# One change to a fused attention and two-MLP kernel: the weights' sign bit, the opening's dates, and one block's transposes

## The chip, the cores and the metric

One Trainium2 chip, one core. The time is the device time of one execution in microseconds (us); the kernel before takes 892.35 us, the median of three runs (892.18 to 892.69).

## What is computed

Sliding-window attention over q, k, v of shape 4 x 8 x 576 x 64 in float32, then two MLPs on the 2304 x 512 result. The weights arrive as float64 and all arithmetic is float32.

```python
# attention: window 64, causal
scores = q @ k.T / 8; scores outside 0 <= i - j < 64 are -1e9
x = softmax(scores) @ v                       # to 2304 x 512
g = max(x @ w_in, 0) + log1p(exp(-abs(x @ w_in)))     # softplus, d_ff 2048
x = g @ w_out
y = (sigmoid(x @ w_gate) * (x @ w_val)) @ w_out2      # d_ff 1536
```

## The kernel before, in words

**Tiling.** The tokens of the first MLP come in five blocks of 512, 384, 384, 512 and 512 (`BLOCKS1`, L21). Attention is done in groups of 64 queries with their 128 keys, all 8 heads at once; block 0 has eight groups, block 1 six. While the first MLP works on block b, the attention of block b + 1 is done between its matmuls. The second MLP runs afterwards over two halves of 768 + 768 tokens with a seven-product (Strassen-like) scheme (L512, L541).

**Precision.** A float32 operand is split into a high part (a rounded fp32r copy) and a low part (the difference), and each product is three matmuls (`mm3`, L405 to L408).

**Weights.** A float64 weight arrives as two 32-bit words. `w_scale` (L160) reads the high word as a float32 and multiplies it by 2^-112 on ScalarE, which moves the exponent into range; `w_shift` (L163) shifts left by 3 on VectorE, which loses the sign; `w_sign` (L167) ors the sign bit of the high word back in on VectorE; `w_low` (L172) ors in the top 3 bits of the low word. `w_hi` (L177, ScalarE) and `w_lo` (L184, VectorE or GpSimd) make the split. The first two weights are converted singly (128x512), later ones in pairs (128x1024).

**Attention.** `att_scores` (L282, TensorE), `att_max` (L294, VectorE), `att_exp` (L310, ScalarE), `att_sum` (L320, VectorE), `att_norm` (L328, GpSimd). Then the probabilities have to be turned so that keys lie on partitions. Near groups (`att_transpose` L334, `att_copy` L364) do it with four TensorE transposes into PSUM and a copy by ScalarE or VectorE. Far groups (`att_blocks` L344, `att_send` L351, `att_fetch` L356) do it with VectorE's transposes of 32x32 blocks, one DMA of 256 KB to DRAM and four DMAs of 64 KB back, all on SyncE's queue. `FAR = 2` (L26) says that blocks 2, 3 and 4 are far; blocks 0 and 1 are near. `att_values` (L381), `att_hi` and `att_lo` (L393, L399) end a group; from block 1 on two groups share one of these.

**Order.** TensorE's order is a list of slots (L601 to L626): projection and output products in turn. Everything else is an event with a slot and a rank (`at`, L631). From the start up to the second MLP a planner (`lead_in`, L957) puts all events in order: it gives each a due time, worked back from what needs it (L971 to L983), then at each step takes, among the events that could start within a window of the soonest one, the one with the earliest due time (L1009). The window is `NEAR` before `OPEN` (34 us, the planned start of the first projection) and `SLACK` after. The eight groups of block 0 are due 2.9 us apart, ending at `OPEN` (L979). The order is fixed when the kernel is built: each engine takes its instructions in that order and waits for semaphores. `warm` (L412) are idle bf16 matmuls that are placed while TensorE waits in the opening; the first projection comes behind all of them (L909).

Of the kernel before, what the change touches and what calls it, by code (L numbers as in the profile page):

```python
# [9 lines left out]
F32 = mybir.dt.float32  # L10
# [3 lines left out]
AF = mybir.ActivationFunctionType  # L14
ALU = mybir.AluOpType
# [7 lines left out]
LAG = 2  # L23
LEAD = 7
COMBO0, COMBO = 36, 9.8
FAR = 2  # L26
TWO = 1
RG = 1.1
HURRY = 1.0
SLACK, NEAR = 0.15, .3  # L30
OPEN = 34.0
FLYING, SWITCH, MARGIN, FLIP, LATE = 10, 1.3, 1.5, 6.0, 2.0
EITHER, HALVES = (("pool", 1.29), ("dve lock", 0.69)), (("pool", 0.75), ("dve lock", 0.42))
# [9 lines left out]
def tile_kernel(ctx: ExitStack, tc: tile.TileContext, qk, vt, w1, w2, wg, wv, wo, out):  # L43
# [20 lines left out]
    nc = tc.nc  # L64
# [50 lines left out]
    pair_t, raw_t, bits_t, w_t = {}, {}, {}, {}  # L115

    def pair(slot, turn, dtype, *shape):
        key = slot // 2, turn
        if key not in pair_t:
            pair_t[key] = wpool.tile([P, 2, *shape], dtype, tag=f"w{slot // 2}", name=f"w{slot // 2}", bufs=1)  # L120
        return pair_t[key]

    def size(i):
        return 2 if 1 < i < WO_AT else 1
# [13 lines left out]
    def raw(i, k):  # L138
        r = raw_t[i - i % 2].rearrange("p c (n two) -> p c n two", two=2)
        return r[:, i % 2:i % 2 + size(i), :, k]  # L140

    def bits(i):
        if i == 1:
            bits_t[i] = bits_t["first"][:, 1:]
        if i not in bits_t:
            u, n = i // 2, size(i)
            if u < 3:
                t = main.tile([P, 2, DM], U32, tag="g", name="bits", bufs=GB)
                bits_t.setdefault("first", t)
            elif 4 <= u < 14:  # L150
                slot = 14 + u % 4 // 2 if u < 12 else 15
                t = pair(2 * slot, -20 - u // 2, U32, 2 * DM)[:, u % 2].rearrange("p (c n) -> p c n", c=2)
            else:
                t = main.tile([P, 2, DM], U32, tag="bits", name="bits", bufs=1)
            bits_t[i] = t[:, :n]
        return bits_t[i]
# [1 line left out]


    def w_scale(i):  # L160
        nc.scalar.activation(out=bits(i).bitcast(F32), in_=raw(i, 1).bitcast(F32), func=AF.Copy, scale=2.0 ** -112)

    def w_shift(i):  # L163
        t = bits_t[i]
        nc.vector.tensor_scalar(out=t, in0=t, scalar1=3, scalar2=None, op0=ALU.logical_shift_left)

    def w_sign(i):  # L167
        t = bits_t[i]
        nc.vector.scalar_tensor_tensor(out=t, in0=raw(i, 1), scalar=0x80000000, in1=t, op0=ALU.bitwise_and,
                                       op1=ALU.bitwise_or)  # L170

    def w_low(i):  # L172
        t = bits_t[i]
# [71 lines left out]
    NG0 = BLOCKS1[0] // Q  # L245
# [128 lines left out]
    def both(g):  # L374
        return (g - 1, g) if grp_block[g][0] >= TWO else (g,)
# [255 lines left out]
    def at(slot, order, fn, *args):  # L631
        events[slot].append((order, len(events[slot]), fn, args))
# [28 lines left out]
    def attention(g, t, far):  # L661
        at(t, 20, att_scores, g)
        at(t + 1, -30, att_max, g)
        at(t + 2, -30, att_exp, g)
        near, odd = g < NG0, g % 2
        at(t + 4 - near, -33, att_sum, g)
        at(t + 4 - near, -32, att_norm, g)
        if far:
            at(t + 5 + 2 * odd, -31, att_blocks, g)
            at(t + 6 + 2 * odd, -61, att_send, g)  # L670
            at(t + 9 + 2 * odd, -61, att_fetch, g)
            e = t + 13
        else:
            e = t + 6 if near else t + 8
            at(e - 2, 21, att_transpose, g)
            at(e - 1, -31, att_copy, g)
        at(e - 4, -59, v_load, g)
        if ends(g) == g:
            at(e, 22, att_values, g)
            at(e + 1, -29, att_hi, g)  # L680
            at(e + 1, -28, att_lo, g)

    for b in range(1, NB1):
        s0, s1 = pos[m1_proj, b - 1, 0], pos[m1_proj, b, 0]
        ng, g0 = BLOCKS1[b] // Q, starts1[b] // Q
        for j in range(ng):
            far = b >= FAR
            first = -3 if far else 9
            t = s0 + first + (s1 - s0 - (14 if far else 15 + first)) * (j // 2) // max(ng // 2 - 1, 1)
            attention(g0 + j, t, far)  # L690
            at(t - 4, -60, qk_load, g0 + j)


    def weight(i, t):
        for k in range(size(i)):
            at(t - 2, 50, w_load, i + k)
        at(t, -20, w_scale, i)
        at(t + 1, -20, w_shift, i)
        at(t + 1, -19, w_sign, i)
        at(t + 1, -18, w_low, i)  # L700
        at(t + 2, -20, w_hi, i)
        for k in range(size(i)):
            at(t + 2, -19, w_lo, i + k)

    for i in (0, 1, *range(2, len(seq1), 2)):
        weight(i, i + LAG - (i < 3) * (3 - i) - LEAD)
# [3 lines left out]
    def used_last(slot):  # L710
        return max(pos[m1_proj if kind == "w1" else m1_out, NB1 - 1, f]
                   for (kind, f), _ in seq1[slot - slot % 2:slot - slot % 2 + 2])

    for f in range(NF2):
        t, i = COMBO0 + int(COMBO * f), len(seq1) + 2 * f
        at(t - 2, -60, w_load, i)
        at(t - 1, -60, w_load, i + 1)
        at(t, -20, w_scale, i)
        at(t + 1, -20, w_shift, i)
        at(t + 1, -19, w_sign, i)  # L720
        at(t + 1, -18, w_low, i)
        at(t + 3, -15, c_sums, f)
        at(t + 4, -15, c_sum4, f)
        for k, part in enumerate(("a", "v", "x", "s4")):
            at(t + 2 + k, -14, c_hi, f, part)
            at(t + 2 + k, -13, c_lo, f, part)
            at(t + 6 + k, -61, c_send, f, part)
    for f in range(NF2):
        i = WO_AT + f
        t = end + (-7, -1)[f] if f < 2 else pos[m2_out, 0, f - 2, 0] - 1  # L730
        t0 = t - 8
        assert used_last(place[i]) < t < pos[m2_out, 0, f, 0] - 4, (f, used_last(place[i]), t, pos[m2_out, 0, f, 0])
        at(t0, -60, w_load, i)
        at(t, -20, w_scale, i)
        at(t + 1, -20, w_shift, i)
        at(t + 2, -20, w_sign, i)
        at(t + 3, -20, w_low, i)
        at(t + 4, -20, w_hi, i)
        at(t + 4, -19, w_lo, i)
    at(last + 4, -62, wc_load, 0, 0)  # L740
    at(end, -62, wc_load, 0, 1)
    for s in range(NS2):
        t = last + 2 if s == 0 else pos[m2_prod, s - 1, 3, 0]
# [5 lines left out]
    for k in range(7):  # L749
        for kc in range(2):  # L750
            t = max(used_last(2 * k + kc) + 1, last + 18 + k)
# [26 lines left out]
    first = -int(RG * NG0) - 6  # L778
    for g in range(NG0):
        t = int(first + RG * g)  # L780
# [13 lines left out]
    def turned(g):  # L794
        return (att_blocks if grp_block[g][0] >= FAR else att_transpose, g)

    def traits(fn, a, *rest):
# [48 lines left out]
        if fn is att_hi:  # L848
            b, off = grp_block[a]
            b, off = grp_block[both(a)[0]]  # L850
# [20 lines left out]
            return "act", 0.12 + 0.48 * size(a), deps, ring  # L871
        if fn is w_shift:
            return "dve lock", 0.15 + 0.27 * size(a), [(w_scale, a)], []
        if fn in (w_sign, w_low):
            return "dve lock", 0.15 + 0.54 * size(a), [(w_shift if fn is w_sign else w_sign, a)], []
        if fn is w_hi:
            deps, u = [(w_low, a)], a // 2
            if a >= WO_AT:
# [65 lines left out]
    def order_of(deps_of):  # L944
        seen, out = set(), []

        def visit(key):
            if key not in seen:
                seen.add(key)
                for d in deps_of[key]:  # L950
                    visit(d)
                out.append(key)
        for key in deps_of:
            visit(key)
        return out

    def lead_in():  # L957
        nodes, when = {}, []
        for i, (fn, b, *_) in enumerate(slots[:end]):
            ng = BLOCKS1[b + 1] // Q if b + 1 < NB1 else 0  # L960
            when.append(when[-1] + gap if when else OPEN)
            gap = 12 * (BLOCKS1[b] / 2400 + 0.0137) + 2.05 * ng / (2 * NF1)
        for t in sorted(events):
            if t < end:
                us = when[t] if t >= 0 else OPEN + 2.9 * t
                for order, n, fn, args in sorted(events.pop(t), key=lambda e: e[:2]):
                    nodes[fn, *args] = [us + order / 400, *traits(fn, *args)]
        deps_of = {k: [d for d in nodes[k][3] if d in nodes] for k in nodes}
        after = {k: [d[:-1] for d in nodes[k][3] if d[-1] is None] for k in nodes}
        due = {}  # L970
        for key in reversed(order_of(deps_of)):  # L971
            fn, a, *_ = key
            rank, kind, us, _, _ = nodes[key]
            if kind in CHOICES:
                us = kind[0][1]
            near = fn in (qk_load, v_load) and a < NG0 or fn.__name__.startswith("att") and a < NG0
            if near or fn.__name__.startswith("w_") and a < NSLOT:
                if fn is att_lo:
                    due[key] = min(due.get(key, OPEN), OPEN - 2.9 * (NG0 - 1 - a))  # L979
                us = 2 + us / 400 if kind == "sp" else us + 0.1  # L980
                nodes[key][0] = due[key] - us - HURRY * (fn.__name__.startswith("w_")) * max(0, a - 16) / 14
            for d in deps_of[key]:
                due[d] = min(due.get(d, 1e9), nodes[key][0])  # L983
# [3 lines left out]
        while todo:  # L987
# [21 lines left out]
            start, _, n, key, kind, us = min((r for r in ready if r[0] < soonest + (NEAR if soonest < OPEN else SLACK)), key=lambda r: r[1:])  # L1009
# [80 lines left out]
```

## Time and profile before

| | us |
|---|---|
| median of three runs | 892.35 |
| profiled execution, its own time | 892.14 |
| its span, first to last instruction | 890.3 |
| TensorE busy | 882.0 |
| VectorE busy | 522.9 |
| ScalarE busy | 398.2 |
| GpSimd busy | 154.7 |

The span is 1.84 us shorter than the execution's own time, and that execution is 0.21 us under the median. A busy TensorE in this table is a sum over matmuls whose ends are modelled; whether it ever waits is read from its waits, not from this share.

### The profile page before, as it was taken

How to read it: one execution, taken by the hardware profiler on the slowest of the kernel's cores; microseconds unless marked ns; L12 is line 12 of the kernel's file. 1: busy time of each engine (PE TensorE's matmuls, PEld its weight loads, DVE VectorE, ACT ScalarE, POOL GpSimd, SP SyncE). 2: the span in 40 equal slices, each digit the busy share in tenths (PEclk: the TensorE clock that was granted, in tenths of full speed). 3: DMA queues.
4: the chain of work that ended last, by engine and by line, in shares of the span. 5: the costliest groups of instructions: out<-in, count | busy, mean ns of one | idle time of the engine just before them, and what ended most of it. 6: DMA issues, size and time to landing. Idle time of an engine off the chain costs nothing.

```text
span 890.3 us, 13467 instructions
## 1 busy us (share of the span) xinstructions
PE 882.0 (99%) x5035; PEld 795.9 (89%) x5035; DVE 522.9 (59%) x907; ACT 398.2 (45%) x878; POOL 154.7 (17%) x157
## 2 busy tenths in 40 slices
PE   9999999999999999999999999999999999999997
PEld 7788889999999888888889999999999999999996
DVE  5899976556646657365515667667445447444444
ACT  6867866537755656245323333334222225122222
POOL 4001201102110121003001233331111112111110
PEclk9999999999999999999999999999999999999999
DMA  9946446657886764773306665545454445444441
GB/s 349 396 160 219 136 161 219 244 171 248 270 267 229 234 229 157 229 261 131 131 18 242 243 252 206 201 179 212 185 204 156 156 157 221 173 166 166 166 166 72
DMA packets 56209, 177.57 MB, mean 199 GB/s; under 512 B 6096, under 2 KB 21456, under 8 KB 51536
## 3 DMA queue, kind: packets, MB, share of 16 engines
q1 hardware_dynamic: 56000, 176.58, 56.0%
q8 instruction: 40, 0.66, 0.3%
q14 instruction: 25, 0.20, 0.1%
q10 hardware_dynamic: 144, 0.13, 0.0%
HBM read 139.72 MB, written 36.96 MB: 198 GB/s over the span
## 4 chain that ended last, share of the span: by engine, by line
PE 93%; DMA 4%; DVE 2%; ACT 1%; issue 0%; SPq 0%; ACTq 0%
PE h L406 17%; PE h L408 17%; PE h L407 17%; PE acc L406 11%; PE acc L407 11%; PE acc L408 11%; PE at L290 2%; PE at L408 2%; PE at L407 2%; PE at L406 2%; PE at L388 2%; DMA raw<-in_w 1%; DMA w<-in_w 1%; DMA w<-in_vt 1%; DMA w<-in_qk 1%; DVE w L174 0%
## 5 line engine op out<-in xcount | busy, mean ns | idle before, releaser
L524 DVE TENSOR_TENSOR w<-h,w 128x384 f32<-128x384 f32 x216 | 117.1, 556 | 160.1 <-PE h L408 157.4
L406 PE MATMUL h<-w,wc 128*128 128x384 f32 x504 | 169.0, 335 | 0.1
L408 PE MATMUL h<-w,wc 128*128 128x384 f32 x504 | 169.0, 335 | 0.0
L407 PE MATMUL h<-w,wc 128*128 128x384 f32 x504 | 168.8, 335 | 0.0
L536 POOL TENSOR_TENSOR g<-w,g 128x384 fp32r<-128x384 f32 x70 | 74.0, 1057 | 296.8 <-ACT g L529 252.1
L406 PE MATMUL h<-xt,w 128*128 128x512 f32 (+1 forms) x320 | 119.1, 372 | 0.4 <-ACT w L180 0.3
L406 PE MATMUL acc<-g,w 128*128 128x512 f32 (+1 forms) x320 | 119.4, 373 | 0.0
L408 PE MATMUL h<-xt,w 128*128 128x512 f32 (+1 forms) x320 | 117.9, 368 | 0.5 <-DVE w L188 0.5
L408 PE MATMUL acc<-g,w 128*128 128x512 f32 (+1 forms) x320 | 117.6, 368 | 0.0
L407 PE MATMUL acc<-g,w 128*128 128x512 f32 (+1 forms) x320 | 117.6, 368 | 0.0
L407 PE MATMUL h<-xt,w 128*128 128x512 f32 (+1 forms) x320 | 117.6, 368 | 0.0
L448 DVE TENSOR_TENSOR g<-h,g 128x512 fp32r<-128x512 f32 (+1 forms) x80 | 50.7, 633 | 83.3 <-ACT g L442 82.9
L406 PEld LDWEIGHTS h<-w,wc 128*128 128x128 f32 x504 | 94.6, 188 | 2.3 <-DVE w L524 0.4
L407 PEld LDWEIGHTS h<-w,wc 128*128 128x128 f32 x504 | 94.6, 188 | 2.0
L408 PEld LDWEIGHTS h<-w,wc 128*128 128x128 f32 x504 | 94.6, 188 | 0.0
L529 ACT CAST g<-w 128x384 fp32r<-128x384 f32 x72 | 36.9, 513 | 119.1 <-DVE w L524 119.1
L435 ACT ACTIVATE h<-h 128x512 f32<-128x512 f32 (+1 forms) x80 | 43.2, 540 | 104.6 <-PE h L408 104.3
L408 PEld LDWEIGHTS h<-xt,w 128*128 128x128 f32 x320 | 60.1, 188 | 8.9 <-DVE w L188 1.4
L406 PEld LDWEIGHTS h<-xt,w 128*128 128x128 f32 x320 | 60.1, 188 | 8.6 <-issue 0.6
L331 POOL TENSOR_TENSOR p<-p,st 128x512 f32<-128x512 f32 (+1 forms) x28 | 29.2, 1049 | 220.8 <-DVE st L326 107.6
L406 PEld LDWEIGHTS acc<-g,w 128*128 128x128 f32 x320 | 60.1, 188 | 7.7
L408 PEld LDWEIGHTS acc<-g,w 128*128 128x128 f32 x320 | 60.1, 188 | 7.5
(129 smaller groups left out, 1433.6 us busy)
## 6 DMA issues: line engine op xcount, KB each, us to landing
wc<-wcd SPq DMA_DIRECT2D x36, 1792.0 KB, 7.4
qk<-in_qk SPq DMA_DIRECT2D x28, 512.0 KB, 4.9
wcd<-raw SPq DMA_DIRECT2D x24, 512.0 KB, 3.2
w<-in_w SPq DMA_DIRECT2D x16, 512.0 KB, 9.2
raw<-in_w SPq DMA_DIRECT2D x16, 512.0 KB, 4.6
v<-in_vt SPq DMA_DIRECT2D x25, 256.0 KB, 3.6
raw<-in_wg SPq DMA_DIRECT2D x12, 512.0 KB, 5.1
raw<-in_wv SPq DMA_DIRECT2D x12, 512.0 KB, 6.7
```

The source lines that it names most:

```text
L290: nc.tensor.matmul(out=s[:, j, :w], lhsT=t[:, 0, j, :], rhs=t[:, 1, j, :w], start=g >= NG0, stop=g >= NG0 or j == NPAIR - 1)
L331: nc.gpsimd.tensor_tensor(out=p[:, :, :w], in0=p[:, :, :w], in1=st[:, 2, :].unsqueeze(2).to_broadcast([P, NPAIR, w]), op=ALU.mult)
L388: nc.tensor.matmul(out=o[h * Q:(h + 1) * Q, j, k * Q:(k + 1) * Q], lhsT=v[:w, (2 * j + h) * Q:(2 * j + h + 1) * Q], rhs=pt[:w, h, j], star ...
L406: nc.tensor.matmul(out=o, lhsT=lh, rhs=rh, start=first, stop=False)
L407: nc.tensor.matmul(out=o, lhsT=lh, rhs=rl, start=False, stop=False)
L408: nc.tensor.matmul(out=o, lhsT=ll, rhs=rh, start=False, stop=last)
L435: nc.scalar.activation(out=t, in_=t, func=AF.Softplus)
L448: nc.vector.tensor_tensor(out=g[:, 1, :n], in0=t, in1=g[:, 0, :n].bitcast(F32), op=ALU.subtract)
L524: nc.vector.tensor_tensor(out=out, in0=a, in1=b, op=op)
L529: nc.scalar.copy(out=g[:, 0, :HALF], in_=t)
L536: eng.tensor_tensor(out=g[:, 1, :HALF], in0=t, in1=g[:, 0, :HALF].bitcast(F32), op=ALU.subtract)
```

## The change

- `w_scale` uses the activation `Prelu` instead of `Copy`, with a slope of -2^32 for negative inputs. A negative weight w becomes |w| x 2^-80, and a positive one stays w x 2^-112. The two differ by 32 in the exponent field, and the shift by 3 moves that bit into the sign position. `w_sign` and its three places in the events are gone, so that `w_low` follows `w_shift`.
- `FAR` is 1: block 1's six groups are turned by VectorE and the queue as well. The slots of block 1's groups keep their start (9) and are spread over two slots less (17 instead of 15 in the formula), and their values come 13 slots after the scores instead of 8.
- The groups of block 0 are due 2.0 us apart instead of 2.9, and `NEAR` is 0.1 instead of 0.3.

```diff
-FAR = 2
+FAR = 1
-SLACK, NEAR = 0.15, .3
+SLACK, NEAR = 0.15, .1
 def w_scale(i):
-    nc.scalar.activation(..., func=AF.Copy, scale=2.0 ** -112)
+    nc.scalar.activation(..., func=AF.Prelu, scale=2.0 ** -112, alpha=-2.0 ** 32)
-def w_sign(i):
-    t = bits_t[i]
-    nc.vector.scalar_tensor_tensor(out=t, in0=raw(i, 1), scalar=0x80000000, in1=t, op0=ALU.bitwise_and,
-                                   op1=ALU.bitwise_or)
             far = b >= FAR
-            first = -3 if far else 9
-            t = s0 + first + (s1 - s0 - (14 if far else 15 + first)) * (j // 2) // max(ng // 2 - 1, 1)
+            first = -3 if b > 1 else 9
+            t = s0 + first + (s1 - s0 - (14 if b > 1 else 17 + first)) * (j // 2) // max(ng // 2 - 1, 1)
-        at(t + 1, -19, w_sign, i)
...
-                    due[key] = min(due.get(key, OPEN), OPEN - 2.9 * (NG0 - 1 - a))
+                    due[key] = min(due.get(key, OPEN), OPEN - 2.0 * (NG0 - 1 - a))
```

## Rows read from the trace of the kernel before

**Rows 1.** The page: the span, and each engine's busy time.
```profile
span 890.3 us, 13467 instructions
PE 882.0 (99%) x5035; PEld 795.9 (89%) x5035; DVE 522.9 (59%) x907; ACT 398.2 (45%) x878; POOL 154.7 (17%) x157
```
**Rows 2.** TensorE's waits from 30 us to the end: total, times, longest.
```profile
PE h L408 <- DVE w L188: 0.5, 1, 0.5
PE h L406 <- ACT w L180: 0.3, 1, 0.3
```
**Rows 3.** TensorE's timeline: the two matmuls that waited (start, duration, line, wait before).
```profile
37.79 0.50 PE L406 MATMUL h<-xt,w 128*128 128x512 f32 x1 [0.26 <-ACT w L180]
...
93.38 0.50 PE L408 MATMUL h<-xt,w 128*128 128x512 f32 x1 [0.53 <-DVE w L188]
```
**Rows 4.** Stretches: length, busy PE, PEld, DVE, ACT, POOL, clock, DMA share, GB/s.
```profile
7.00:24.00 17.00, 16.85 (x191) 13.80 (x190) 11.33 (x34) 15.95 (x81) 6.68 (x7) 1.00 1.03 393
24.00:30.00 6.00, 5.55 (x54) 3.03 (x52) 5.54 (x10) 4.98 (x9) 1.18 (x2) 1.00 1.03 407
...
42.00:120.00 78.00, 77.47 (x453) 64.19 (x452) 71.88 (x103) 57.60 (x111) 7.16 (x6) 1.00 0.56 188
```
**Rows 5.** TensorE's timeline, 24 to 31 us: start, duration, line.
```profile
25.82 1.43 PE L388 MATMUL at<-pt,w 128*64 128x64 f32 x32
27.18 2.76 PE L418 MATMUL h<-idle 128*128 128x512 bf16 x12
30.10 0.47 PE L406 MATMUL h<-xt,w 128*128 128x512 f32 x1
```
**Rows 6.** ScalarE's timeline, 23 to 38 us.
```profile
23.07 0.37 ACT L317 ACTIVATE w<-acc,st 128x128 f32<-128x128 f32 x1
...
26.82 0.69 ACT L161 ACTIVATE bits<-w 128x512 f32<-128x512 f32 x1
27.41 0.62 ACT L180 CAST w<-bits 128x512 fp32r<-128x512 f32 x1
27.91 0.38 ACT L397 CAST xt<-at 128x256 fp32r<-128x256 f32 x1
...
34.30 1.28 ACT L435 ACT_TABLE_LOAD   x1
...
36.69 1.05 ACT L180 CAST w<-bits 128x1024 fp32r<-128x1024 f32 x1
```
**Rows 7.** VectorE's timeline, 25 to 35 us.
```profile
25.50 0.69 DVE L169 SCALAR_TENSOR_TENSOR bits<-w,bits 128x512 uint32<-128x512 uint32 x1
...
28.01 0.69 DVE L169 SCALAR_TENSOR_TENSOR bits<-w,bits 128x512 uint32<-128x512 uint32 x1
...
29.22 0.41 DVE L402 TENSOR_TENSOR xt<-at,xt 128x256 fp32r<-128x256 f32 x1
...
30.76 1.22 DVE L169 SCALAR_TENSOR_TENSOR bits<-w,bits 128x1024 uint32<-128x1024 uint32 x1
...
32.89 1.22 DVE L174 SCALAR_TENSOR_TENSOR bits<-w,bits 128x1024 uint32<-128x1024 uint32 x1
```
**Rows 8.** The chain that ended last: one of six like pieces in block 0.
```profile
107.24 0.44 PE at L339 x4
```
**Rows 9.** TensorE's timeline: the last of these transposes, values, the next block's first projection.
```profile
107.08 0.60 PE L339 MATMUL at<-ident,p 128*128 128x128 f32 x4
...
114.46 1.15 PE L388 MATMUL at<-pt,v 128*64 128x64 f32 x32
...
127.47 0.33 PE L406 MATMUL h<-xt,w 128*128 128x384 f32 x1
```
**Rows 10.** VectorE: block transposes, whole span; sign steps (L169) alone, 24 to 120 us.
```profile
L347 DVE STREAM_TRANSPOSE pd<-p 128x512 f32<-128x512 f32 x20 | 14.0, 700 | 4.3 <-DMA pd<-pd 3.5 <-POOL p L331 0.8
...
24.00:120.00 96.00, 18.81 (x16) 1.00 0.64 229
```
**Rows 11.** DMA issues: count, KB each, median us from issue to landing.
```profile
pt<-pd SPq DMA_DIRECT2D x84, 64.0 KB, 2.6
pd<-pd SPq DMA_DIRECT2D x20, 256.0 KB, 3.3
```

More of the change, by code (lines that the diff above doesn't have):

```diff
@@ L160, in w_scale @@
     def w_scale(i):
-        nc.scalar.activation(out=bits(i).bitcast(F32), in_=raw(i, 1).bitcast(F32), func=AF.Copy, scale=2.0 ** -112)
+        nc.scalar.activation(out=bits(i).bitcast(F32), in_=raw(i, 1).bitcast(F32), func=AF.Prelu, scale=2.0 ** -112,
+                             alpha=-2.0 ** 32)
     def w_shift(i):
@@ L719, in tile_kernel @@
         at(t + 1, -20, w_shift, i)
-        at(t + 1, -19, w_sign, i)
         at(t + 1, -18, w_low, i)
@@ L735, in tile_kernel @@
         at(t + 1, -20, w_shift, i)
-        at(t + 2, -20, w_sign, i)
         at(t + 3, -20, w_low, i)
@@ L873, in traits @@
             return "dve lock", 0.15 + 0.27 * size(a), [(w_scale, a)], []
-        if fn in (w_sign, w_low):
-            return "dve lock", 0.15 + 0.54 * size(a), [(w_shift if fn is w_sign else w_sign, a)], []
+        if fn is w_low:
+            return "dve lock", 0.15 + 0.54 * size(a), [(w_shift, a)], []
         if fn is w_hi:
```

## The prediction

> **What bounds the kernel now.** The page gives TensorE 99% of the span [rows 1], but a busy share can hide waits, so the next view is TensorE's own waits. From 30 us to the end there are two: 0.5 us for a low half of a weight and 0.3 us for a high half [rows 2, 3]. So from its first projection at 30.10 us [rows 5] the kernel is TensorE's list of matmuls, one after the other, and only three things can shorten it: fewer matmuls, those 0.8 us, and an earlier first projection. An engine that gets lighter beside that is worth nothing by itself.
>
> The stretches [rows 4] show what the other engines do meanwhile. From 7 to 24 us ScalarE is the fullest beside the transfers (15.95 of 17.00 us; it does the eight groups' exponentials), and the DMA engines are full (share 1.03, 393 GB/s). From 42 to 120 us VectorE has 71.88 of 78.00 us busy: it is not the bound, as TensorE waits for it once, but it is near it. The DMA share there is 0.56.
>
> How the first projection gets its start is in the three timelines. The last exponential begins at 23.07 [rows 6]; the last values end at 27.25, then come twelve idle matmuls of 2.76 us, to 29.94, and then the projection [rows 5]. Beside them ScalarE scales and rounds weights (26.82, 27.41) before it rounds the last group (27.91 to 28.29) [rows 6], and VectorE does two sign steps (25.50, 28.01) and a low half before the last group's low half, which ends at 29.63 [rows 7]. So two things end within 0.3 us of each other: the idle matmuls, and VectorE's queue.
>
> **The transposes.** Six groups of block 1 lose four transposes each on TensorE. In the chain such a piece takes 0.44 us [rows 8]; the timeline gives the same four 0.60 us [rows 9] since it counts the last one's modelled end. The next matmul begins before that end, so I take the 0.44: 6 x 0.44 = 2.6 us, all of it on the path, and 6 x 0.60 = 3.6 us as the other end. That is the firmest term: those instructions leave an engine that does not wait.
>
> In their place come six of VectorE's block transposes, 0.70 us each [rows 10], six transfers of 256 KB (3.3 us to landing) and 24 of 64 KB (2.6 us) [rows 11], and six copies out of PSUM go. I cost these at nothing, and what hides them is the following. On VectorE the sign steps pay for them: sixteen of them take 18.8 us between 24 and 120 us [rows 10], against 6 x 0.70 = 4.2 us more. The queue carries 188 GB/s in that stretch against 407 in the opening [rows 4]; the added 12 x 256 KB = 3.1 MB would take 7.7 us of the 78 at the opening's rate. For latency: in a pair the two groups share one VectorE tile, so I put them in series, 0.70 + 3.3 us to send the first, 0.70 + 3.3 to send the second and then its four fetches, for which I take 2.6 us and as much again for issuing: 13.2 us in all. Before, it was the transposes' 0.60 us [rows 9] and a copy, which I put at the 0.62 us of a rounding of the same shape [rows 6], 1.2 us, so the values can come some 12 us later. The last pair's values begin at 114.46 and block 1's first projection at 127.47 [rows 9], 13.0 us apart, and rounding a pair's values takes about 1.6 us of it (twice a single group's 0.38 and 0.41 [rows 6, 7]). That leaves 11.4 us, just short of 12; but the new slots also put the last pair's scores two slots earlier, and a slot is 12 matmuls of 512 columns, 2.7 us at the pace of the twelve idle ones [rows 5], 5.4 in all, so about 5 us of slack are left. GpSimd's normalising stays as it is. If that cover goes, TensorE waits in its order with everything of block 1 behind it. On SyncE's queue a send waits for VectorE and a fetch for the send's landing, and weight loads issued behind them wait too; the weights of this stretch are the ones that VectorE converts a few us later, so the first sign would be a projection that waits for `w_lo`.
>
> **The sign step.** Removed: one VectorE instruction for each conversion, 0.69 us for a single weight and 1.22 for a pair [rows 7, 10]. Of all these, only those ahead of a TensorE wait count. The wait of 0.3 us at 37.79 [rows 3] is for the first pair: its sign step ran at 30.76, its low bits at 32.89 to 34.11, too late for ScalarE, which took a table load at 34.30 and rounded the pair only at 36.69 [rows 6, 7]. Without 0.69 + 0.69 + 1.22 us on VectorE the low bits are there about 2.6 us earlier, near 31.5, ahead of the table load, so this wait goes. The 0.5 us wait at 93.38 [rows 3] is also at the end of a full VectorE queue, and 1.22 us for each conversion is more than it. I take both, 0.8 us; the ends are 0.8 and 0, should a later stall take their place. Later sign steps (the second MLP's weights) lie beside TensorE and give nothing. On ScalarE the scaling stays one pass; the trace has no Prelu, so its cost is bounded by the nearest rows: 0 to, say, 0.1 us more than the 0.69 us scaling, hidden except twice in the opening.
>
> **The opening.** Both ends of the opening move: VectorE loses 1.4 us of sign steps before the last group's low half, and the closer dates with the narrower window change the order of all that stands before it. The trace can't show the new order, so I bound it. If the last group went straight through from its values (27.25, then 0.38 on ScalarE, 0.41 on VectorE and some hand-over), the projection would begin near 28.2, 1.9 us earlier, provided the idle matmuls are not all behind the values. If the roundings of earlier groups, 0.38 us each like the last one [rows 6], moved behind the exponentials too, three of them give another 1.1: 3 us is the far end. At the other end the twelve idle matmuls stay where they are and nothing is gained, or the last group meets a weight step more on ScalarE (0.69 + 0.62 us [rows 6]) and it is 1 us later. I take 1.0 us earlier, about half way between standing still and the straight passage, since both VectorE and ScalarE have something to shift but the idle matmuls bind at 29.94 anyway. That 1.0 is my least certain term.
>
> **Sum.** 2.6 + 0.8 + 1.0 = 4.4 us off the profiled execution's 892.14 us, that is 887.7; the median stands 0.2 above that execution, so 887.9.
>
> **Rivals.** *The opening gives nothing or costs.* The idle matmuls hold the first projection at 30.1, or the new order ends a little later. For it: the two ends at 29.94 and 29.63. Against: the dates of the last group stay, those of the earlier ones move later, so nothing passes ahead of the last group that did not before. Time: 892.35 - 3.4 = 888.9, and up to 1.5 us more, 890.4, still faster; only with a wait left over too would it be within 0.2%.
>
> *The round trip is late.* If transfers take twice the 13.2 us in this stretch, the last pair comes 26.4 - 1.2 = 25 us after where it came before, against 11.4 + 5.4 = 17 us of room: 8 us of wait less what the other terms give, 892.35 - 4.4 + 8 = 896; at half that excess, 892. For it: the two-step path has never run in block 0, beside weight loads. Against: 20 such sends at 3.3 us [rows 11], and TensorE never waited for one [rows 2]. The Trainium skill ("VectorE: DVE Perf Modes", The three transpose paths) warns that a plain DMA copy that transposes by strides is 19 times slower than the crossbar's 1309 ns; by an estimate from that page a group's turn would take 25 us, about 50 for a pair, and this rival would be the outcome at over 900. The trace disagrees: here the blocks are turned by VectorE first and a fetch lands in 2.6 us [rows 11].
>
> *Slower: the new activation brings table loads.* If Prelu is not in the table that is loaded, each scaling brings a load before it and one back, 2 x 1.28 us [rows 6]. ScalarE has 1.0 us free from 24 to 30 us [rows 4], and two scalings stand before the first two projections: 5.1 us, with the first pair behind them another 2.6. That makes 892.35 - 2.6 + 7.7 = 897; it decides from three loads on. Against: the scaling by Copy runs under both the exponentials' and the softplus table in this kernel with no load of its own. The Trainium skill ("ScalarE: Activation LUTs", Table sets) says that cheap functions stand in every set but does not name this one; no run so far shows it.
>
> *The change does not do what it says* would be transposes still on TensorE in block 0; the diff leaves no path for that.
>
> **Chances.** The forecast 0.66; the opening without gain 0.20, of which about nine tenths is still faster; the round trip late 0.09, about two thirds of it near no change; table loads 0.05. About 0.2% (1.8 us) can be told from no change here. Faster 0.84, the same 0.09, slower 0.07. The range: down to 3.6 + 0.8 + about 2.5 off (885.4), up to the transposes alone with an opening 1 us later (892.35 - 2.6 + 1.0 = 890.8), so 885.4 to 890.8.
>
> **What would show it.** Right: no transposes on TensorE after the opening; the first projection near 29; no or shorter waits of TensorE for weights; VectorE clearly under 92% from 42 to 120 us; block 1's first projection at about 123 instead of 127.47. Wrong: a wait of TensorE for the fetched tile, ScalarE table loads that end in a scaling, or a first projection after 31.

## The result and the profile after

The changed kernel takes **898.17 us** (median of four runs, 897.19 to 900.46), against 892.42 us for the kernel before (four runs, 892.18 to 892.69): a ratio of **1.0068, 95% interval 1.0049 to 1.0087**. It is 5.7 us slower; 4.5 us faster had been forecast. The profiled execution took 897.19 us.

The page first, against [rows 1]:

```profile
span 895.2 us, 13454 instructions
PE 881.2 (98%) x5011; PEld 794.5 (89%) x5011; DVE 480.4 (54%) x875; ACT 435.0 (49%) x902; POOL 150.7 (17%) x156
```

TensorE has 24 instructions less, as the diff says, and VectorE is 42.5 us lighter. But ScalarE, which should have got a like-for-like instruction and lost some copies out of PSUM, went from 398.2 to 435.0 us: 36.8 us more. It has 24 instructions more (eight copies are gone, so 32 are new), and they lead to the next view: ScalarE's groups, of which these are the table loads (line, count, total and mean duration, idle time before). First the kernel before:

```profile
L435 ACT ACT_TABLE_LOAD x15 | 19.2, 1283 | 0.3
L317 ACT ACT_TABLE_LOAD x14 | 18.0, 1283 | 0.8 <-DVE st L307 0.5
L1030 ACT ACT_TABLE_LOAD x1 | 1.3, 1283 | 0.7 <-PEq L1077 0.7
L550 ACT ACT_TABLE_LOAD x1 | 1.3, 1283 | 0.0
```

And after:

```profile
L431 ACT ACT_TABLE_LOAD x31 | 39.8, 1283 | 0.5
L161 ACT ACT_TABLE_LOAD x20 | 25.7, 1283 | 11.1 <-DMA raw<-in_wv 10.4 <-DMA raw<-in_wg 0.4
L313 ACT ACT_TABLE_LOAD x10 | 12.8, 1283 | 3.0 <-DVE st L303 2.9
L1023 ACT ACT_TABLE_LOAD x1 | 1.3, 1283 | 0.7 <-PEq L1070 0.7
L546 ACT ACT_TABLE_LOAD x1 | 1.3, 1283 | 0.0
```

31 loads have become 63 (the expectations below count 64). L435 before and L431 after are the same step, the softplus; its loads double. L161 is the scaling: no load ended in it before, twenty do now. ScalarE's timeline (start, duration, line) shows where, and where not:

```profile
22.20 0.21 ACT L313 ACTIVATION_READ_ACCUMULATOR w<-acc,st 128x1 f32 x1
...
22.66 0.68 ACT L161 ACTIVATE bits<-w 128x512 f32<-128x512 f32 x1
...
33.05 1.28 ACT L431 ACT_TABLE_LOAD   x1
...
37.62 1.28 ACT L161 ACT_TABLE_LOAD   x1
38.91 2.22 ACT L161 ACTIVATE w<-raw 128x1024 f32<-128x1024 f32 x2
...
62.27 1.28 ACT L161 ACT_TABLE_LOAD   x1
63.56 1.15 ACT L161 ACTIVATE w<-raw 128x1024 f32<-128x1024 f32 x1
64.73 1.28 ACT L431 ACT_TABLE_LOAD   x1
66.03 0.58 ACT L431 ACTIVATE h<-h 128x512 f32<-128x512 f32 x1
66.64 0.59 ACT L438 CAST g<-h 128x512 fp32r<-128x512 f32 x1
67.24 1.28 ACT L161 ACT_TABLE_LOAD   x1
```

In the opening the Prelu follows the exponentials and needs no load (22.66 and up to 30.94). From 37.62 on, where the softplus (L431) has put its own table in, each scaling between two softplus, or each run of scalings (two at 38.91), costs one load on the way out and one on the way back, 1.28 us each. Prelu itself is no slower: 1.15 us here for 128x1024, and Copy took 1.13 to 1.17 us on average for that shape before.

TensorE's waits from 30 us on were 0.5 and 0.3 us [rows 2]. After, they are these, beside 0.2 us behind the idle matmuls (what waited, what ended it, total, times, longest):

```profile
PE h L402 <- DVE g L444: 3.2, 1, 3.2
PE h L402 <- ACT xt L393: 1.6, 1, 1.6
PE h L403 <- DVE xt L398: 1.2, 1, 1.2
PE acc L402 <- ACT x L462: 0.6, 1, 0.6
```

The longest is at 86.59. The chain that ended last, followed back from there, says what VectorE was late for:

```profile
77.08 1.06 ACT w L176
78.16 1.28 ACT L313
...
79.77 2.90 ACT p L313 x15
82.69 0.77 DVE st L321
...
84.19 1.04 DVE w L170
...
85.86 0.69 DVE g L444
86.59 0.75 PE h L402
```

The wait is booked on VectorE, but the chain runs over ScalarE: exponentials of block 1 behind a table load, their sum on VectorE (which waited for them), then the low bits of a weight, then the low half of the softplus result, which TensorE needs. The load at 78.16 is not one of the new ones; a run below has it too, 6.3 us earlier. What makes the chain late lies ahead of it, in loads such as those at 62.27, 64.73 and 67.24. The second place is block 1's start, where the rounded attention output (ACT, L393) is late. And after the longest wait, and after the two at block 1's start, TensorE went on at half speed for a while. The stretches (length, busy PE, PEld, DVE, ACT, POOL, clock, DMA share, GB/s):

```profile
86.60:89.70 3.10, 3.10 (x7) 2.43 (x8) 2.96 (x5) 1.56 (x2) 0.00 (x0) 0.51 0.55 176
131.60:134.10 2.50, 2.50 (x9) 2.50 (x8) 1.52 (x4) 1.85 (x3) 0.97 (x2) 0.50 0.71 267
```

A granted clock of 0.51 and 0.50 is the 1.2 GHz level of the two. Here TensorE counts as busy all the time, and only the clock column shows the loss.

### The profile page after: what moved, and what is told of

Same layout as the page of the kernel before. It is cut to its first block, busy times and chain, and to the rows that moved or that the text cites. A ratio compares the mean times of both kernels' runs of the same rounds, so it can differ in the third digit from the quotient of the medians.

```text
span 895.2 us, 13454 instructions
## 1 busy us (share of the span) xinstructions
PE 881.2 (98%) x5011; PEld 794.5 (89%) x5011; DVE 480.4 (54%) x875; ACT 435.0 (49%) x902; POOL 150.7 (17%) x156
## 4 chain that ended last, share of the span: by engine, by line
PE 84%; ACT 6%; DMA 5%; DVE 3%; issue 1%; SPq 0%; DVEq 0%; ACTq 0%
PE h L402 16%; PE h L403 15%; PE h L404 15%; PE acc L402 9%; PE acc L404 9%; PE acc L403 9%; PE at L286 2%; PE at L404 2%; PE at L403 2%; PE at L402 2%; PE at L384 2%; DMA raw<-in_wv 1%; ACT L431 1%; DMA w<-in_w 1%; ACT w L176 1%
## 5 line engine op out<-in xcount | busy, mean ns | idle before, releaser
L402 PE MATMUL h<-xt,w 128*128 128x512 f32 (+1 forms) x320 | 120.7, 377 | 5.0 <-DVE g L444 3.2
L403 PE MATMUL h<-xt,w 128*128 128x512 f32 (+1 forms) x320 | 119.1, 372 | 1.2 <-DVE xt L398 1.2
L404 PE MATMUL h<-xt,w 128*128 128x512 f32 (+1 forms) x320 | 118.7, 371 | 0.0
L431 ACT ACTIVATE h<-h 128x512 f32<-128x512 f32 (+1 forms) x80 | 43.2, 540 | 101.0 <-PE h L404 100.7
L402 PEld LDWEIGHTS h<-xt,w 128*128 128x128 f32 x320 | 60.9, 190 | 13.5 <-DVE g L444 3.4
L558 ACT ACTIVATE w<-w 128x384 f32<-128x384 f32 x36 | 18.9, 526 | 105.2 <-DVE w L520 105.1
L403 PEld LDWEIGHTS h<-xt,w 128*128 128x128 f32 x320 | 61.1, 191 | 8.7 <-DVE xt L398 1.4
L404 PEld LDWEIGHTS h<-xt,w 128*128 128x128 f32 x320 | 61.1, 191 | 7.8
L402 PEld LDWEIGHTS acc<-g,w 128*128 128x128 f32 x320 | 60.1, 188 | 8.8 <-ACT x L462 1.1
```

Source lines behind the costliest of these rows:

```text
L402: nc.tensor.matmul(out=o, lhsT=lh, rhs=rh, start=first, stop=False)
L403: nc.tensor.matmul(out=o, lhsT=lh, rhs=rl, start=False, stop=False)
L404: nc.tensor.matmul(out=o, lhsT=ll, rhs=rh, start=False, stop=last)
L431: nc.scalar.activation(out=t, in_=t, func=AF.Softplus)
L558: nc.scalar.activation(out=sb, in_=u2, func=AF.Sigmoid)
```

## The experiments

Three theories for the 5.7 us. **Loads**: Prelu is not in the softplus's table, and the loads delay what stands behind them on ScalarE. **Turning**: block transposes and the round trip of block 1 are late, whatever the sign step does. **Opening**: the closer dates cost something. A run's "sign step" below is the VectorE instruction that ors the sign in.

**The other two parts, with the old scaling.** Kernel before with this edit:

```diff
-FAR = 2
+FAR = 1
-SLACK, NEAR = 0.15, .3
+SLACK, NEAR = 0.15, .1
-            first = -3 if far else 9
+            first = -3 if b > 1 else 9
...
-OPEN - 2.9 * (NG0 - 1 - a)
+OPEN - 2.0 * (NG0 - 1 - a)
```

> The changed kernel with the scaling by Copy and the sign step put back; block 1 stays turned by VectorE and the queue, and the new dates stay. Table theory (each Prelu between two softplus activations makes ScalarE load a table before it and another after it, and the chain ScalarE, VectorE, TensorE becomes the bound): the 33 added table loads go, the waits of TensorE after 30 us (6.6 us in sum) go, and the time is 887 to 889 us, about what was forecast without any gain of the sign step. Turning theory (block 1's exponentials and round trip come at a bad place, and VectorE's queue stands behind them): the wait of 3.2 us near 83 us stays and the time is 895 to 899 us.

Measured: 896.33 us, ratio 1.0038 (1.0023 to 1.0053), with 31 loads. So taking Prelu away, with its loads, does not bring the forecast's time as long as the sign step is back on VectorE. TensorE's waits and the stretch:

```profile
PE acc L408 <- DVE w L188: 2.9, 1, 2.9
PE h L408 <- DVE w L188: 2.4, 2, 1.4
...
42.00:120.00 78.00, 72.62 (x382) 59.18 (x381) 69.91 (x102) 51.92 (x100) 5.78 (x6) 0.98 0.60 201
```

The longest are VectorE's, for low halves of weights (L188; two for ScalarE make 0.9 us more, and one of 0.4 us stands at 321.83 in a later block's values): VectorE has sign steps and block transposes both. The loads theory alone had failed at this point, and the turning theory stood.

**The scaling alone.** Kernel before with Prelu, without the sign step:

```diff
-func=AF.Copy, scale=2.0 ** -112)
+func=AF.Prelu, scale=2.0 ** -112, alpha=-2.0 ** 32)
-        at(t + 1, -19, w_sign, i)
...
```

> The kernel before with only the Prelu in and the sign step out; block 1 is turned on TensorE, the dates are the old ones. Table theory: about 30 more table loads than before, ScalarE over 85% busy from 42 to 120 us, TensorE waits by several us: 895 to 902 us. Turning theory: VectorE is lighter, the waits of 0.8 us go, 890.5 to 892 us.

Measured: 899.27 us, ratio 1.0075 (1.006 to 1.009), 69 loads. The scaling alone brings as much as the whole change, with block 1 turned by TensorE as before; its longest wait, 3.4 us, is for a copy on ScalarE (L364). So the turning theory by itself failed too.

**Only another function.** Kernel before, one word changed; the sign step stays, so nothing is saved:

```diff
-func=AF.Copy
+func=AF.Abs
```

> The kernel before with the scaling by Abs in place of Copy, and nothing else: the shift drops the sign anyway and the sign step puts it back, so the work and the order are those of before, and only the function's table can differ. Table theory, if Abs is like Prelu missing from softplus's table: about as many loads as with Prelu, VectorE as full as before, and so at least as slow as the Prelu alone, 896 to 906 us. If instead the Prelu instruction itself is the trouble, or the missing sign step moves the order: no added loads, 892 to 893 us.

Measured: 904.75 us, ratio 1.0132 (1.0113 to 1.0151), 69 loads. Twelve us for one word: each instruction of the source is the same, in number and size. ScalarE's loads in this run:

```profile
L435 ACT ACT_TABLE_LOAD x34 | 43.6, 1283 | 0.6
L161 ACT ACT_TABLE_LOAD x21 | 26.9, 1283 | 21.7 <-DMA raw<-in_wv 19.7 <-issue 1.7
```

This is a plain price of 38 more loads on the kernel before. The Trainium skill ("ScalarE: Activation LUTs", Table sets) counts abs among the cheap functions that every set has; by that this run would have stayed at 892. The measurement decides: Abs got loads like Prelu.

**The planner is told.** Changed kernel, where the order's planner takes the scaling as a step of the exponentials' kind, so that it charges a switch of tables:

```diff
-            return "act", 0.12 + 0.48 * size(a), deps, ring
+            return "act exp", 0.12 + 0.48 * size(a), deps, ring
```

> The changed kernel, with the planner told that the scaling needs the exponentials' table, so that it charges 1.3 us for a change and gathers what needs the same one. Table theory: clearly fewer loads than the 64 of the changed kernel, less waiting, 889 to 896 us. Turning theory: the time stays at 896 to 899 us.

Measured: 893.17 us, ratio 1.0009 (0.9999 to 1.0019), 67 loads. That the loads would get fewer had been expected, and they did not; 5.0 us of time went all the same. So the number of loads does not set the time by itself. TensorE's waits still sum to 6.0 us, the longest 1.5, but the granted clock is 1.00 from 42 to 140 us, where the changed kernel fell to 0.51 and 0.50, and the first projection is at 28.98 instead of 29.59. That it counts what stands behind a load, and that the planner now leaves room for it, is my reading; no run singles it out.

**The whole change without the loads.** Changed kernel with Copy in place of Prelu, everything else in the same order; it leaves out the signs of the weights.

```diff
-func=AF.Prelu, scale=2.0 ** -112, alpha=-2.0 ** 32)
+func=AF.Copy, scale=2.0 ** -112)
```

> The changed kernel with Copy in place of Prelu and still no sign step, so that the weights lose their signs: the same instructions in the same order on every engine but for the table loads. Theory one (the loads are all of the loss; without them VectorE has the room that the block transposes need): the loads of ScalarE fall from 64 to about 31, no wait of TensorE over 0.5 us after 30 us, 887 to 889 us. Theory two (turning block 1 through the queue costs by itself, whatever the engines' loads): 891 to 896 us, with a wait of 1 us or more near 83 to 95 us.

Measured: **886.7 us, ratio 0.9935 (0.992 to 0.995)**. Against the changed kernel, 898.17 - 886.7 = **11.5 us is what the loads cost**. The lost signs change the numbers computed but no step; the run with Abs, which keeps the signs, shows a cost of loads too. TensorE's matmuls come in the same order in both traces. Its page, the stretch to set beside [rows 4], its two first projections, and from ScalarE's timeline the rounding and the load that began the chain above at 77.08 and 78.16:

```profile
PE 877.2 (99%) x5009; PEld 793.0 (90%) x5011; DVE 481.6 (54%) x875; ACT 394.3 (45%) x870; POOL 150.8 (17%) x156
...
42.00:120.00 78.00, 78.00 (x448) 65.00 (x447) 67.01 (x103) 58.68 (x113) 7.10 (x7) 1.00 0.70 233
...
29.35 0.47 PE L401 MATMUL h<-xt,w 128*128 128x512 f32 x1
...
122.34 0.33 PE L401 MATMUL h<-xt,w 128*128 128x384 f32 x1
...
70.83 1.05 ACT L175 CAST w<-w 128x1024 fp32r<-128x1024 f32 x1 [1.89 <-DVE w L169]
71.89 1.28 ACT L312 ACT_TABLE_LOAD   x1
```

32 instructions fewer on ScalarE, 40.7 us less: 32 x 1.283 = 41.1. TensorE is busy for all of the 78 us, at clock 1.00. ScalarE reaches the rounding ahead of block 1's exponentials 6.3 us earlier (70.83 against 77.08), and TensorE has no wait after 30 us. The transposes gone from TensorE, the sign steps gone from VectorE, the round trip in time: that is what the forecast had assumed, and the time lies in its range.

**The turning alone**: kernel before with `FAR = 1` and the two slot formulas only.

```diff
-FAR = 2
+FAR = 1
-            first = -3 if far else 9
+            first = -3 if b > 1 else 9
...
```

> The kernel before with block 1 turned by VectorE and the queue and its new slots; the scaling by Copy, the sign step and the old dates stay. If the block transposes on a VectorE that is already full are what costs in the run with Copy and sign step: TensorE waits for low halves of weights by 3 us or more and runs slowly after, 894 to 898 us. If it was the new dates: 889 to 891 us.

Measured: 896.34 us, ratio 1.0046 (1.0028 to 1.0065). VectorE's timeline ahead of the longest wait, and the matmul that waited:

```profile
87.82 0.28 DVE L325 TENSOR_SCALAR st<-st 128x4 f32<-128x4 f32 x1 [0.96 <-ACT p L317]
...
88.23 0.70 DVE L347 STREAM_TRANSPOSE pd<-p 128x512 f32<-128x512 f32 x1
88.85 1.22 DVE L165 TENSOR_SCALAR w<-w 128x1024 uint32<-128x1024 uint32 x1
89.99 0.68 DVE L188 TENSOR_TENSOR w<-w,w 128x512 fp32r<-128x512 f32 x1
...
90.73 0.50 PE L408 MATMUL acc<-g,w 128*128 128x512 f32 x1 [2.97 <-DVE w L188]
```

Nothing waits for a fetched tile: the round trip is in time here too. TensorE pays for the place of the low half (89.99) in VectorE's queue: ahead of it stand 0.96 us of waiting for block 1's exponentials, the block transpose of 0.70 us and a shift. Which of these is too much, no run singles out.

**The dates alone**: kernel before with the closer dates and the narrower window.

```diff
-SLACK, NEAR = 0.15, .3
+SLACK, NEAR = 0.15, .1
...
-OPEN - 2.9 * (NG0 - 1 - a)
+OPEN - 2.0 * (NG0 - 1 - a)
```

> The kernel before with the closer dates and the narrower window alone. If the block transposes cost: the first projection begins 0.5 to 1 us earlier than at 30.10 and the waits stay near 0.8 us, 891 to 892.2 us. If the dates cost: 894 us or more, with waits for the first weights of several us.

Measured: 892.59 us, ratio 1.0001 (0.9991 to 1.001). The first projection came at 29.77 instead of 30.10; nothing of it reaches the end (block 1's first projection is at 127.75, against 127.47), and nothing is lost by it. The time lies a little above the first of the two ranges.

**The sign step alone**: kernel before without it, and without the sign (left out), scaling by Copy.

```diff
-        at(t + 1, -19, w_sign, i)
...
```

> The kernel before without its sign step, with nothing in its place, so that the weights lose their signs: what the missing sign step is worth by itself. As forecast: the 0.8 us of waits go, and the opening moves by 0 to 0.5 us: 891 to 891.8 us. If the planner's new order has a cost of its own: 892.5 us or more. Beside the run with only the Prelu (899.27) it gives what the table loads cost there.

Measured: 891.12 us, ratio 0.9985 (0.9975 to 0.9995). TensorE has no wait after 30 us. Set beside the scaling alone with Prelu, 899.27, the loads cost 8.2 us in this order of steps.

**Prelu only where the exponentials' table is in.** From the kernel with the other two parts: the weights 0 to 7 are scaled by Prelu, the others by Copy with the sign step.

```diff
+def SIGNED(i):
+    return i < 8
...
+        signed = {} if not SIGNED(i) else {"alpha": -2.0 ** 32}
...
+             func=AF.Prelu if signed else AF.Copy, scale=2.0 ** -112, **signed)
...
+        if not SIGNED(i):
+            at(t + 1, -19, w_sign, i)
```

> Block 1 turned by VectorE and the queue and the new dates, with Prelu and no sign step only for the first five conversions (weights 0 to 7), which ScalarE does before its first softplus, while the exponentials' table is loaded; Copy and sign step for all later ones. The built program has as many table loads as the kernel before, 31. If a Prelu costs only its loads, it costs nothing here, and VectorE is spared 2 x 0.69 + 3 x 1.22 = 5.0 us before 42 us: the waits for low halves that the run with Copy and sign step had near 90 to 120 us (5.4 us) shrink by about that, 888 to 891 us. If Prelu itself costs, or the relief comes too early to reach 90 us: 894 us or more.

Measured: 892.57 us, ratio 1.0001 (0.9992 to 1.001), 31 loads: between the two ranges, and 3.8 us better than with the sign step everywhere. TensorE still waits for low halves (2.7 us in three waits); the sign steps beside block 1's transposes are still there, and that they are the reason is my reading.

**Two more, where the planner puts them beside exponentials.** As above, with:

```diff
-    return i < 8
+    return i < 8 or i in (16, 18)
-            return "act", 0.12 + 0.48 * size(a), deps, ring
+            return "act exp" if SIGNED(a) else "act", 0.12 + 0.48 * size(a), deps, ring
```

> As the run with the early Prelus, and two more (weights 16 and 18), which the planner is told to put beside the exponentials; again 31 loads in the built program. 2.4 us less on VectorE shortly before the waits near 90 us: 887 to 890 us, no later than the early Prelus alone. If the planner's tie of scalings to exponentials makes weights late, waits of TensorE for ScalarE's rounding or scaling show up, 891 us or more.

Measured: 890.37 us, ratio 0.9974 (0.9962 to 0.9985), again 31 loads: just above the range of 887 to 890. The waits for low halves are 1.9 us.

**The same, and GpSimd helps.** Low halves of the first MLP's weights may go to GpSimd too:

```diff
-            return EITHER if a >= WO_AT else ALONE, 0, [(w_hi, a - a % size(a))], []
+            return EITHER, 0, [(w_hi, a - a % size(a))], []
```

> As the run with placed Prelus, and the low halves of the first MLP's weights may be made by GpSimd where the planner finds that sooner, as it already does for later weights. If VectorE's room alone decides: 886.5 to 889 us, no waits left. If GpSimd's slower subtraction (1.29 against 0.69 us) or its hold on VectorE costs more than it frees: 890 us or more.

Measured: **888.67 us, ratio 0.9962 (0.9949 to 0.9975)**: below both kernels, and it leaves nothing out. Its interval overlaps that of the run before it, so the two are not told apart. Its profile is of an execution of 891.37 us, 2.7 above the median. The stretch, and the wait for low halves, down from 1.9 us; four other waits make 1.9 us there, so "no waits left" did not come out:

```profile
42.00:120.00 78.00, 77.63 (x422) 64.79 (x422) 68.61 (x96) 54.41 (x103) 17.40 (x13) 1.00 0.67 220
...
PE h L416 <- DVE w L196: 0.4, 1, 0.4
```

**GpSimd's help with the sign step everywhere**: the first experiment with that same line.

```diff
-            return EITHER if a >= WO_AT else ALONE, 0, [(w_hi, a - a % size(a))], []
+            return EITHER, 0, [(w_hi, a - a % size(a))], []
```

> The run with Copy and sign step (block 1 turned by VectorE and the queue, new dates), with the low halves of the first MLP's weights allowed on GpSimd: another way to give VectorE room, with no Prelu at all. If a full VectorE is what makes the turning cost: 888 to 893 us, below the 896.3 without it. If the turning costs by the place of its steps: 895 us or more.

Measured: 895.39 us, ratio 1.0031 (1.002 to 1.0043): 0.9 us below the run without GpSimd's help, with overlapping intervals. GpSimd was busy for 18.0 us of the stretch, but VectorE got no lighter by it: 71.12 us of the 78, against 69.91. It made 16 low halves instead of 23, yet in the largest groups one took 795 ns instead of 682, and the low bits of a pair 1399 instead of 1219. So this run doesn't test what room on VectorE alone would give.

## Why the prediction was wrong

**The step that failed** is in the part on the sign step: "On ScalarE the scaling stays one pass; the trace has no Prelu, so its cost is bounded by the nearest rows: 0 to, say, 0.1 us more". The pass itself was bounded rightly. What it brings along was not: 32 loads, 41 us of ScalarE, 11.5 us of the time. The rival had the mechanism ("a load before it and one back") and nearly the time (897 against 898.17), but a chance of 0.05, with the argument that Copy ran under both tables without a load. That row is about Copy. It says nothing of a function that the trace does not have, and the text had said itself that the trace has none. The upper end of the bound should have held two loads for each place.

**Its place** was wrong as well. The rival put the loads in the opening, where they never came, as Prelu ran behind the exponentials without one. They fall from 37 us on. So its 897, added up from six loads in the opening, is near the result by luck. Between the changed kernel and the one without the loads, the 11.1 us of span are: 0.24 at the first projection (29.59 against 29.35); the waits of 3.2, 1.6, 1.2 and 0.6 us; and twice 1.6 us for the slower clock. The last is worked out from TensorE's timelines: after the wait at 86.59 twelve matmuls take 4.45 us, to 91.04, and the same twelve without the loads take 2.82 (82.85 to 85.67); at block 1's start eleven take 3.56 (131.09 to 134.65) against 1.93 (122.52 to 124.45). That makes 10.1 us. The last 1.0 is in the waits: the view counts a wait from the modelled end of the matmul before. Between the starts of the same matmuls in both traces, the four cost 3.5, 1.8, 1.4 and 0.8 us, 7.5 in all instead of 6.6.

**The other terms**, read without the loads. From the first projection to block 1's first it was 127.47 - 30.10 = 97.37 us [rows 5, 9]. Without the sign step it is 95.83 (from 30.13 to 125.96). In the view, these are the first two lines; the next two are matmuls of that run near 91 us, and the last is from the kernel before, ahead of its longer wait:

```profile
30.13 0.47 PE L401 MATMUL h<-xt,w 128*128 128x512 f32 x1
...
125.96 0.33 PE L401 MATMUL h<-xt,w 128*128 128x384 f32 x1
...
91.32 0.40 PE L402 MATMUL h<-xt,w 128*128 128x512 f32 x1
91.56 0.40 PE L403 MATMUL h<-xt,w 128*128 128x512 f32 x1
...
92.46 0.40 PE L407 MATMUL h<-xt,w 128*128 128x512 f32 x1
```

Those 1.54 us stand against the 0.8 that the two waits had been given, since a wait is longer from start to start here too: 92.46 to 93.38 [rows 3] is 0.92 us, and 91.32 to 91.56 is 0.24 for the same two matmuls without the sign step, 0.68 more where the view books 0.53. The other parts take it on to 122.34 - 29.35 = 92.99, another **2.84 us; the forecast for the transposes was 2.6**. Between the two projections both traces have the same matmuls, but for the 24 transposes. The opening was to give 1.0: 0.75 without the loads, 0.51 with them, 0.33 for the dates alone. The idle matmuls do bind there, as the forecast chose. Together it forecast 4.4 us; without the loads it is 5.8. The three terms make 5.1 of that, and the rest, after block 1's first projection, was not followed up.

**The cover was real.** The prediction costed the block transposes at nothing, with the sign steps named as what is to "pay for them". The turning alone shows the price where that cover is missing: 3.8 us slower. That it is VectorE's room, and not the order which the planner makes of it, is argued from its timeline. And it shows why one can't add parts here: alone the sign step is worth 1.4 us, the turning -3.8, the dates 0, which sums to 2.4 slower, while all three without the loads are 5.8 faster. With block 1 on VectorE, the sign step's going is worth 896.33 - 886.7 = 9.6 us.

**The late round trip** did not occur: in the changed kernel, without the loads and with the turning alone, no matmul that reads a fetched tile waits after 30 us. In the changed kernel the median fetch landed in 2.9 us and the median send of 256 KB in 2.4, far from the 25 us that had been estimated for a group's turn by strides. The one such wait for a transfer in all the runs is 0.2 us, with GpSimd's help and the sign step everywhere; three other runs have one of 0.3 to 0.7 us at a later block's values, booked on VectorE. **VectorE under 92%** and **block 1's first projection at about 123** were put down as signs of success; both are there without the loads (67.01 of 78, 122.34). With them VectorE is less busy still, 58.97 of 78 us, and late all the same: what it waits for most is ScalarE's rounding of the softplus result (5.7 us in seven waits in that stretch) and of weights (3.6 in three). The sign named for failure, "ScalarE table loads that end in a scaling", is the one that was seen.

## What to carry to other kernels

A new activation function is priced by the table that is loaded when it runs, not by its own pass: before taking it, list which functions run just before and after each place, and give a function that the trace has never shown two loads per place as its upper bound. Where it costs loads in some places only, use it there only: Prelu for the few weights that come beside the exponentials kept the loads at 31 and, with GpSimd's help, gave 888.67 us. When an edit moves work onto an engine that another edit empties, measure them together; alone, each is something else.

## What the runs showed of the hardware

Prelu and Abs both got a load beside the softplus (63 and 69 loads in all, against 31), and Copy none; Prelu got none behind the exponentials (22.66 to 30.94 in the changed kernel). A load took 1.28 us, and the next activation began 1.29 us after the load did (62.27 to 63.56), so there is no further gap to see; the Trainium skill ("ScalarE: Activation LUTs", What ACT_TABLE_LOAD costs) adds a drain of about 1.4 us, which these rows don't show.

A wait that the view books at 3.2 us on TensorE cost 5.1: 3.5 from start to start, and 1.6 while the granted clock was 0.51, in the three microseconds that followed it. Behind the wait of 2.97 us with the turning alone the clock was 0.51 from 91.8 to 94.2; with the planner told, waits of up to 1.5 us left it at 1.00. So a wait of a full TensorE can be worth more than its length.
